# Left-side tile addresses, an opening with both pairs in turn, and a single reciprocal pass

## The chip, the core and the metric

The kernel runs on one core of one Trainium2 chip. The metric is the time of one execution on the device in microseconds (us). A core has a TensorE (matmul, "PE", with its weight loads listed apart as "PEld"), a VectorE ("DVE"), a ScalarE ("ACT"), a GpSimd ("POOL") and a SyncE ("SP"). SP and POOL issue most transfers here: what stands in one of these queues is issued in order, so a load that has to wait for its buffer holds up all loads behind it. Each engine, too, works through its own instructions in the order in which they were written.

## What is computed

`x` is 2048 x 640 in float32. A linear-attention block with 32 heads of 20 columns and a gated feed-forward block with 1536 inner columns are mixed row by row.

```python
def _A_ref(x, wqkv, wo):
    ...
    phi = lambda t: jnp.where(t > 0, t + 1, jnp.exp(t)) + 1e-6
    pq, pk = phi(q), phi(k)
    kv = jnp.einsum("bhsd,bhse->bhde", pk, v)
    z = jnp.einsum("bhsd->bhd", pk)
    num = jnp.einsum("bhqd,bhde->bhqe", pq, kv)
    den = jnp.einsum("bhqd,bhd->bhq", pq, z)[..., None] + 1e-6
    o = num / den
    return (lambda x, *d: x.transpose(*d))(o, 0, 2, 1, 3).reshape(B, S, D) @ wo

def _B_ref(x, w_gate, w_up, w_down):
    ...
    h = _sigmoid(g) * u
    return jnp.einsum("bsf,fd->bsd", h, w_down)

x = A_x
g = _sigmoid((x * gate_w).sum(-1, keepdims=True))
a = _A_ref(x, A_wqkv, A_wo)
b = _B_ref(x, B_w_gate, B_w_up, B_w_down)
return g * a + (1 - g) * b
```

## The kernel before

Every float32 product is made of three matmuls of rounded operands (`mm3`, lines 190 to 194): high times high, high times low, low times high. So every operand is split first (`split`, line 220): ACT writes the high half, DVE the low half, which is why nearly all instructions of the trace carry the helpers' lines 191 to 193 (PE), 203 (ACT) and 207 (DVE). In the names of the trace `h` and `l` at the end stand for the two halves. The products are formed by a Strassen-like scheme on 2 x 2 blocks with 7 products instead of 8 (the forms B11, B21, T1 to T4, B22).

The 2048 columns are four groups of 512; groups 2 and 3 make up pair 1, groups 0 and 1 pair 0. The work runs in stages:

- **k and the Gram-like sums** (0 to about 144 us), with the tile `gt` at its end.
- **The M stage** (144 to 180), woven into the q products. Heads are taken in six groups (`hg`: five of 120 columns, one of 40). `kv_part` multiplies `gt` with the loaded `wv_sb` and leaves `kvt`, split into `kvh` and `kvl`; `wo_split` splits a group's rows of `wo` into `woh` and `wol`; `m_part` multiplies the two and stores M to `m_dram`, from where the folded weights `mp_dram` are formed. The weights of q and of the feed-forward stage come as raw tiles `wst` (two buffers) through `load_w`, on the same SP queue as `wv_sb` and `wo_sb`.
- **q** (to about 215): its features p are stored to `p_dram`, and their small parts of the sum are made.
- **The feed-forward stage** (215 to 536): twelve steps f of 128 inner columns; both pairs in turn, pair 1 first. `FBlock` multiplies the sigmoid of the gate with the up product and (1 - g), stores the result tiles `c` in `h_dram` and forms their sums T1 to T4 (`turned`, `sums`). In the background the factor g / den is made (`fac_steps`): `den` sums p times z over the rows on DVE, `spread` sums it over the heads by a float32 matmul with `e_mat`, `one` takes the reciprocal, and p times the factor is stored as two further row blocks of `h_dram` and as the remainder `r_dram`. It is done for pair 1 at f=0 and 3, and for pair 0 at f=4 and 8.
- **The last stage** (536 to 766): the down product, in which the attention's p is treated as two more row blocks. A list `SEQ` gives the order of (pair, form); each has four chunks (`hw`, 128 x 1024, split into `hf`) and one set of weights: E (768 columns), O (1280), SE/SO (512 each, sums of E and O made on DVE by `sums` in `queue_down`), L and the remainder `hr` (loaded as `ot<-r`). Results are gathered in eight `ot` tiles and stored by POOL. The sums of the last f step come from `late_sums`, which loads T1, x, B21 and B22 back into four `ot` tiles.

What sets the order: a planner (`Order`) keeps modelled clocks of PE, ACT and DVE. Work for ACT and DVE is queued (`add`) with a cost, a key and a time from which it may run; `fill` emits queued items where the modelled clocks leave room, `need(key)` forces them out, `items` goes before `mid`, and `mid` before `lazy`. `after="p"` first fills and then lets the instruction wait for PE's modelled clock. In the last stage `plan` is the order in which weights (E, O, L, S), chunks (h), `late` and `r` are queued.

Tiles live in pools that grow from the left end or from the right end of the on-chip memory. The left-hand ones (`kp`, `m1`, `p1`, `mp`, `ha`, `pb`, `hb`) stand behind `common`, whose last tile is a placeholder named `space` (line 250) of 32 float32 numbers per partition. In the built program the left-hand operands begin at a multiple of 128 bytes, the right-hand ones (`px`, `pa`, `pg`, `xa`, `pw`, `wa`) at 96 modulo 128. In the last stage the chunks `hf` are on the left and the weights `wa` on the right; in the feed-forward stage pair 0's inputs are partly on the left and pair 1's on the right.

Of the kernel before, what the change touches and what calls it, by code (L numbers as in the profile page):

```python
# [45 lines left out]
class Order:  # L46
# [122 lines left out]
def gated_mix_kernel(ctx: ExitStack, tc: tile.TileContext, xt, xn, wk, wv, wo, wst_q, wst_f, out_t):  # L169
# [74 lines left out]
    h_dram = {(pr, n): dram.tile([P, FC // 2 + 2, TG], F32, name=f"h{pr}{n}") for pr in range(2) for n in FORMS}  # L244
    x_dram = [dram.tile([P, TG], F32, name=f"x{pr}") for pr in range(2)]
# [4 lines left out]
    common.tile([P, 32], F32, name="space")  # L250
# [407 lines left out]

    def load_w():
        if w_loads:  # L660
            n = kind, i = w_loads.pop(0)
            t = pg.tile([P, 2, D], F32, name="wst", tag="wst", bufs=2)
            if kind == "f":
                nc.sync.dma_start(t, wst_f[i, :, 0:2])
            elif kind == "q":
                nc.sync.dma_start(t, wst_q[:, 2 * (i % 2):2 * (i % 2) + 2])
# [389 lines left out]
    def wo_split(hg):  # L1056
        _, w = hg_slice(hg)
        woh = mp.tile([bdn, D], F32R, name="woh", tag="woh", bufs=2)
        wol = mp.tile([bdn, D], F32R, name="wol", tag="wol", bufs=2)
# [4 lines left out]
    def queue_wo(hg):  # L1064
        if hg < NHG:
            order.add(a_cost(D), v_cost(D), lambda: wo_split(hg), ("wo", hg), lambda: MO_AT[hg], first=True)

    def kv_part(hg):
# [3 lines left out]
        for m in range(KC):  # L1072
# [6 lines left out]
        act(kvh[:w, :w], kvt[:w, :w], AF.Copy, "v")  # L1079
        KV[hg] = (kvh, kvl)  # L1080
        order.add(0, v_cost(bdn), lambda: vec2(kvl[:w, :w], kvt[:w, :w], f32(kvh[:w, :w]), OP.subtract), ("kv", hg),
                  first=True)
        load_mv(hg + 3)

    def m_part(hg):
        c0, w = hg_slice(hg)
        order.need(("kv", hg))
# [9 lines left out]
        queue_wo(hg + 2)  # L1097
# [8 lines left out]
    load_mv(2)  # L1106
    load_mo(0)
    load_mo(1)

# [14 lines left out]
    def m_close():  # L1124
# [8 lines left out]
        nt.queue_sums(last=False)  # L1133

# [6 lines left out]
    def gate_row(g):  # L1141
        return l_dram.rearrange("a b -> (a b)")[g * TG:(g + 1) * TG].partition_broadcast(P)
# [28 lines left out]
    queue_wo(1)  # L1171
    queue_wo(0)
# [66 lines left out]
    class FBlock(Block):  # L1239
# [47 lines left out]
        def late_sums(self):  # L1287
# [3 lines left out]
            for n, t in zip(names, tiles):  # L1291
                nc.sync.dma_start(t, h_dram[self.pr, n][:, self.p] if n else x_dram[self.pr])
            self.turned(*tiles, lambda at=order.pe + 16.0: at)


    def fac_steps(pr):

        st = {}
        gs = (2 * pr, 2 * pr + 1)

        def load_pair(n):
            g, u = gs[n // 3], 2 * (n % 3)
            w = min(2, KC - u)
            t = st["b"][:, 2 * (n % 2):2 * (n % 2) + w]
            nc.sync.dma_start(t, p_dram[:, u:u + w, g])
            st[n] = max(order.pe, order.vec) + 6.0

        def den(n, k):
            td = st["a"][:, n // 3]
            p = st["b"][:, 2 * (n % 2) + k % 2]  # L1310
            if k == 0:
                vec1(td, p, zcol[:, 0:1], zeps[:, 0:1], OP.mult, OP.add)
            else:
                vec3(td, p, zcol[:, k:k + 1], td, OP.mult, OP.add)
            if k in (1, 3, 4) and n + 2 < 6:
                load_pair(n + 2)

        def begin():
            st["a"], st["b"] = h_tile(), h_tile()
            load_pair(0)  # L1320
            load_pair(1)
            for n in range(6):
                for k in range(2 * (n % 3), min(2 * (n % 3) + 2, KC)):
                    order.add(0, v_cost(TG), lambda n=n, k=k: den(n, k), ("den", pr), lambda n=n: st[n], lazy=True)

        def spread(n):

            order.need(("den", pr))
            ps = ps_tile("dd")
            td = st["a"][:, n]  # L1330
            nc.tensor.matmul(ps, e_mat, td, start=True, stop=True)
            order.on_pe(4, TG)
            vec1(td, ps, EPS, op0=OP.add, after="p")
            gt_ = st["b"][:, n]
            nc.sync.dma_start(gt_, gate_row(gs[n]))
            at = order.pe + 5.0
            for j in range(4):
                cs = slice(j * P, (j + 1) * P)

                def one(cs=cs):  # L1340
                    order.on_vec(5 * P, "")
                    nc.vector.reciprocal(td[:, cs], td[:, cs])
                order.add(0, 0.85, one, lazy=True)

            def fin():
                act(gt_, gt_, AF.Sigmoid)
                vec2(td, td, gt_, OP.mult, "a")
            order.add(a_cost(TG), v_cost(TG), fin, ("fac", pr, n), lambda: at, lazy=True)

        def load_q(j):  # L1350

            for n in range(2):
                t = st["b"][:, 2 * n:2 * n + 2]
                if j < 2:
                    nc.sync.dma_start(t, p_dram[:, 2 * j:2 * j + 2, gs[n]])
                else:
                    nc.sync.dma_start(t[:, 0], p_dram[:, KC - 1, gs[n]])
            st["at"] = order.pe + 6.0

        def store(name, j, k):  # L1360
            nc.gpsimd.dma_start(h_dram[pr, name][:, FC // 2 + j], st["b"][:, k])

        def scale(j, n, k):
            t = st["b"][:, 2 * n + k]
            vec3(t, t, EPS, st["a"][:, n], OP.add, OP.mult)
            if j == 2:
                nc.gpsimd.dma_start(r_dram[pr][:, n], t)
            elif n == 0:
                store(("B11", "B21")[k], j, k)
            elif k:  # L1370
                store("B22", j, 3)
                st["at2"] = order.pe + 7.0

        def sums(j, k):
            b11, b21, b12, b22 = (st["b"][:, i] for i in range(4))
            name, i, out, x, y = (("T1", 0, b11, b12, b11), ("T3", 2, b12, b22, b12), ("T2", 3, b22, b22, b11),
                                  ("T4", 1, b21, b21, b22))[k]
            sub(out, x, y)
            store(name, j, i)

        def queue_prep():
            for j in range(3):
                order.add(0, 0, lambda j=j: load_q(j), lazy=True)
                for n in range(2):
                    for k in range(2 if j < 2 else 1):
                        order.add(0, v_cost(TG), lambda j=j, n=n, k=k: scale(j, n, k), ("prep", pr), lambda: st["at"],
                                  lazy=True)
                if j < 2:
                    for k in range(4):
                        order.add(0, v_cost(TG), lambda j=j, k=k: sums(j, k), ("prep", pr), lambda: st["at2"], lazy=True)  # L1390

        def two():
            spread(0)
            spread(1)
            queue_prep()

        return [lambda: order.add(0, 0, begin, lazy=True), two]


    hooks = {}  # L1400
    for pr, fs in ((1, (0, 3)), (0, (4, 8))):
        for f, fn in zip(fs, fac_steps(pr)):
            hooks.setdefault(f, []).append(fn)
    PP = (FC // 2 + 2) // 2
# [9 lines left out]
    def raw_down(odd, pp):  # L1414

        if pp < PP - 1:
            f = 4 * pp + odd
            return wst_f[f:f + 3:2, :, 2].rearrange("f p (o c) -> p f o c", c=P)
        return mp_dram[:, odd:odd + 3:2].rearrange("p f (o c) -> p f o c", c=P)

    def load_down(key, t=None):
# [3 lines left out]
        if kind == "S":  # L1425
            v = t[:, :8 * P].rearrange("p (j o c) -> p j o c", j=2, c=P)
            for j in range(2):
                nc.sync.dma_start(v[:, j], raw_down(j, n // 2)[:, n % 2, :4])
# [10 lines left out]
    d_loads = [("E", pp) for pp in range(1, PP)] + [("O", pp) for pp in range(PP)] + [("L", 0)]  # L1439
# [6 lines left out]
    def queue_down(key):  # L1446
# [4 lines left out]

        def sums():
            v = RAW[key][0]
            (e0, e1), (o0, o1) = ((v[:, j, 0::2], v[:, j, 1::2]) for j in range(2))
            add(o1, e1, o1)
            sub(e1, e0, e1)
            sub(e0, o1, e0)
            sub(o0, o0, e0)
# [20 lines left out]
        if kind == "S":  # L1479
            order.add(0, 4 * v_cost(2 * P), sums, None, at)  # L1480
            for j in range(2):
                order.add(a_cost(4 * P), v_cost(4 * P), lambda j=j: s_part(j), ("wa", ("SE", "SO")[j], n // 2))
# [6 lines left out]
    SEQ = [(1, "B11"), (1, "B21"), (1, "T4"), (0, "B11"), (0, "B21")]  # L1489
    SEQ += [(pr, n) for pr in (1, 0) for n in ("T2", "T1", "T3", "B22")] + [(0, "T4")]  # L1490
# [319 lines left out]
```

## Time and profile before

| what | value |
|---|---|
| runs (us) | 771.77, 772.05, 776.09; median 772.05 |
| profiled execution | 772.33 us, of which the profile's span is 770.5 us |
| mean granted clock of TensorE in it | 0.993 |
| matrix engine busy | 97% of the span |
| moved by transfers | 136.06 MB, 177 GB/s in the mean |

The page of the profile gives busy times, the chain of work that ended last, the costliest groups of instructions with their mean duration, and transfers. The prediction quotes from it and from finer views of the same trace: the table of windows (what each engine did in a stretch), the timeline (one row per instruction: start, duration, engine, line, operation, result <- operands, and in brackets the idle time ahead of it with what ended it; rows named SPq are the queue's own waiting and issuing), and the list of waits. Durations of a matmul in the timeline (0.39 us at 512 columns) overlap with the next one; the pace is read from the starts.

These are the two groups with the longest waits on the page's list of groups:

```profile
L191 PE MATMUL cc<-hf,wa 128*128 128x512 f32 x80 | 32.2, 403 | 1.3 <-ACT hf L203 1.3
...
L192 PE MATMUL cc<-hf,wa 128*128 128x512 f32 x80 | 32.3, 404 | 2.1 <-DVE hf L207 2.1
```

### The profile page before, as it was taken

To read this page: it belongs to the slowest core of one execution; us is meant where nothing else is said; L and a number is where in the kernel's file an instruction comes from. 1 tells how busy PE (TensorE), PEld (TensorE's weight loads), DVE (VectorE), ACT (ScalarE), POOL (GpSimd) and SP (SyncE) were. 2 spreads that over 40 slices of the span, in tenths; PEclk is the share of its full clock that TensorE was granted. 3 is DMA by queue.
4 is the path that set the end of the run, shared out by engine and by line. 5 is a ranking of instruction groups with operands and counts; after the bars stand their busy time and mean duration, and the time that the engine had idled before them with its cause. 6 is when DMAs were issued, how large, how long until landed. Compare 5 with 4: busy or idle time off the path is not lost.

```text
span 770.5 us, 9772 instructions
## 1 busy us (share of the span) xinstructions
PE 747.3 (97%) x3560; PEld 624.5 (81%) x3560; DVE 502.1 (65%) x802; ACT 321.5 (42%) x544; POOL 109.1 (14%) x192
## 2 busy tenths in 40 slices
PE   9999999979899999999999999999789998999998
PEld 7999999868687888788888878887567876888886
DVE  4877577765754667678887699776479593544340
ACT  5664545355666333332333234223264454424320
POOL 0210101011211012013131121241100000010000
PEclk9999999999999999999999999999999999999999
DMA  7553536766535423256465335477878567666431
GB/s 255 123 152 70 137 89 185 199 188 196 192 136 198 144 89 129 70 170 237 172 200 209 138 108 187 177 255 238 279 257 278 187 214 254 221 202 213 134 112 69
DMA packets 59909, 136.06 MB, mean 177 GB/s; under 512 B 10238, under 2 KB 23310, under 8 KB 59861
## 3 DMA queue, kind: packets, MB, share of 16 engines
q1 hardware_dynamic: 43109, 85.88, 34.6%
q0 software_dynamic: 16608, 49.43, 19.7%
q8 instruction: 28, 0.46, 0.2%
q14 instruction: 20, 0.16, 0.1%
q10 hardware_dynamic: 144, 0.13, 0.1%
HBM read 87.11 MB, written 44.70 MB: 171 GB/s over the span
## 4 chain that ended last, share of the span: by engine, by line
PE 75%; DMA 8%; DVE 7%; issue 5%; ACT 3%; SPq 1%; POOL 1%; ACTq 0%; DVEq 0%; POOLq 0%
PE cc L192 7%; PE cc L193 7%; PE cc L191 7%; PE rot L191 7%; PE rot L192 7%; PE rot L193 7%; PE ch L192 6%; PE ch L193 6%; PE ch L191 6%; PE dd L193 5%; PE dd L191 5%; PE dd L192 5%; DMA ot<-r 2%; DMA ws<-wst_f 2%; DVE hf L207 2%
## 5 line engine op out<-in xcount | busy, mean ns | idle before, releaser
L207 DVE TENSOR_TENSOR hf<-hw,hf 128x1024 fp32r<-128x1024 f32 x54 | 65.4, 1223 | 59.3 <-ACT hf L203 59.1
L203 ACT ACTIVATE hf<-hw 128x1024 fp32r<-128x1024 f32 x54 | 56.1, 1054 | 60.8 <-PE rot L193 28.9
L207 DVE TENSOR_TENSOR c<-cc,c 128x512 f32<-128x512 f32 x56 | 37.5, 686 | 48.0 <-PE cc L193 43.5
L203 ACT ACTIVATE wG<-wst 128x640 fp32r<-128x640 f32 x17 | 12.4, 736 | 73.9 <-PE dd L193 73.3
L203 ACT ACTIVATE c<-ch 128x512 f32<-128x512 f32 x32 | 19.2, 598 | 57.3 <-PE ch L193 55.3
L191 PE MATMUL dd<-xrh,wG 128*128 128x512 f32 x90 | 35.5, 395 | 0.0
L193 PE MATMUL dd<-xrh,wG 128*128 128x512 f32 x90 | 35.2, 391 | 0.0
L192 PE MATMUL dd<-xrl,wG 128*128 128x512 f32 x90 | 35.2, 391 | 0.0
L192 PE MATMUL cc<-hf,wa 128*128 128x512 f32 x80 | 32.3, 404 | 2.1 <-DVE hf L207 2.1
L207 DVE TENSOR_TENSOR c<-c,om 128x512 f32<-128x512 f32 x48 | 33.2, 692 | 1.7
L193 PE MATMUL dd<-hf,wa 128*128 128x512 f32 x80 | 31.9, 399 | 2.1 <-DVE wa L207 2.1
L191 PE MATMUL dd<-hf,wa 128*128 128x512 f32 x80 | 31.8, 397 | 2.0 <-ACT wa L203 2.0
L191 PE MATMUL cc<-hf,wa 128*128 128x512 f32 x80 | 32.2, 403 | 1.3 <-ACT hf L203 1.3
L191 PE MATMUL cc<-xbh,wS 128*128 128x512 f32 x84 | 32.8, 390 | 0.0
L193 PE MATMUL cc<-xbh,wS 128*128 128x512 f32 x84 | 32.7, 389 | 0.0
L192 PE MATMUL cc<-xbl,wS 128*128 128x512 f32 x84 | 32.7, 389 | 0.0
L1608 POOL DMA_DIRECT2D out_t<-ot x18 | 9.7, 540 | 159.0 <-DVE ot L207 155.5
L193 PE MATMUL cc<-hf,wa 128*128 128x512 f32 x80 | 32.2, 402 | 0.0
L192 PE MATMUL rot<-pkl,xnh 128*128 128x320 f32 x102 | 31.7, 310 | 0.0
L192 PE MATMUL dd<-hf,wa 128*128 128x512 f32 x80 | 31.7, 396 | 0.0
L191 PE MATMUL rot<-pkh,xnh 128*128 128x320 f32 x102 | 31.6, 309 | 0.0
L193 PE MATMUL rot<-pkh,xnl 128*128 128x320 f32 x102 | 31.4, 308 | 0.0
(485 smaller groups left out, 2240.0 us busy)
## 6 DMA issues: line engine op xcount, KB each, us to landing
hf<-p_dram SPq DMA_DIRECT2D x16, 512.0 KB, 4.6
hw<-h1T SPq DMA_DIRECT2D x16, 512.0 KB, 4.6
hw<-h0T SPq DMA_DIRECT2D x16, 512.0 KB, 4.1
wst<-wst_f SPq DMA_DIRECT2D x12, 640.0 KB, 4.2
xst<-xt SPq DMA_DIRECT2D x10, 640.0 KB, 7.5
hw<-h0B SPq DMA_DIRECT2D x12, 512.0 KB, 4.9
h1T<-c POOLq DMA_DIRECT2D x21, 256.0 KB, 2.6
h0T<-c POOLq DMA_DIRECT2D x21, 256.0 KB, 2.8
```

Of the source, the lines that this page charges most:

```text
L191: nc.tensor.matmul(out, l_hi, r_hi, start=first, stop=False, skip_group_check=True)
L192: nc.tensor.matmul(out, l_hi, r_lo, start=False, stop=False, skip_group_check=True)
L193: nc.tensor.matmul(out, l_lo, r_hi, start=False, stop=last, skip_group_check=True)
L203: nc.scalar.activation(out, src, fn, **kw)
L207: nc.vector.tensor_tensor(out, a, b, op=op)
L1608: (eng or nc.gpsimd).dma_start(out_t[o * P:(o + 1) * P, g * TG + c0:g * TG + c1], t[:, c0:c1])
```

## The change

1. **Addresses.** `space` shrinks from 32 to 24 float32 numbers, so that all left-hand tiles stand 32 bytes lower. Of the 2,512 matmuls with 512 columns in the program, 1,218 had one operand at 0 and the other at 96 modulo 128 bytes; after it 4 have differing ones.
2. **M stage ("q's small parts" and the weights).** The second raw weight load of q (`("q", 1)`) is held until the first two `wv_sb` and `wo_sb` loads are issued, and `("u", 0)` until the loads of the last x tiles (`release_w`). `wv_sb` has two buffers instead of three; `woh` and `wol` three instead of two; the splits of `wo` are queued in the order of the groups; `kvh` is cast on DVE instead of ACT.
3. **One factor pass.** `begin` at f=0 and `den_all` at f=3 treat all four groups at once: four spreads into 32 rows each of one tile, four reciprocals in place of sixteen, then the factor is stored (`f_dram`) and loaded again per pair.
4. **Sums of the S weights** are formed in the feed-forward stage (`load_s`, `sum_s`), stored (`s_dram`) and loaded ready-made in the last stage.
5. **Opening of the last stage.** `SEQ` begins with B11 of both pairs in turn: each E weight is used for a chunk of pair 1 and of pair 0. The late loads go on POOL's queue, both pairs' at the opening; x is stored before the last c tiles; the plan has E1, two chunks, E2 and so on. The copies out of psum wait without `fill` (`"q"`), and B21's results come by an ACT copy and an addition.

```diff
+        if "q" in after:
+            t = self.pe
...
-    common.tile([P, 32], F32, name="space")
+    common.tile([P, 24], F32, name="space")
...
+    w_hold, w_skipped = {("q", 1), ("u", 0)}, []
+    def release_w(n):
+        w_hold.discard(n)
+        if w_skipped:
+            w_skipped.pop()
+            load_w()
...
-            v = mp.tile([P, KC, bdn], F32, name="wv_sb", tag="wv_sb", bufs=3)
+            v = mp.tile([P, KC, bdn], F32, name="wv_sb", tag="wv_sb", bufs=2)
...
-        act(kvh[:w, :w], kvt[:w, :w], AF.Copy, "v")
+        vec_copy(kvh[:w, :w], kvt[:w, :w])
+        vec2(kvl[:w, :w], kvt[:w, :w], f32(kvh[:w, :w]), OP.subtract)
...
-                nc.sync.dma_start(t, h_dram[self.pr, n][:, self.p] if n else x_dram[self.pr])
-            self.turned(*tiles, lambda at=order.pe + 16.0: at)
+                nc.gpsimd.dma_start(t, h_dram[self.pr, n][:, self.p] if n else x_dram[self.pr])
+            self.turned(*tiles, lambda at=order.pe + 30.0: at)
...
+    def sum_s(p):
+        e, o = (st["a"][:, 2 + j].rearrange("p (o k c) -> p k o c", k=2, c=P) for j in range(2))
+        (e0, e1), (o0, o1) = ((t[:, 0], t[:, 1]) for t in (e, o))
+        add(o1, e1, o1)
+        sub(e1, e0, e1)
+        sub(e0, o1, e0)
+        sub(o0, o0, e0)
+        nc.gpsimd.dma_start(s_dram[p], st["a"][:, 2:4])
...
+    def den_all():
+        for n in range(NG):
+            spread(n)
+        den_out()
+        queue_s()
+    hooks = {0: begin, 3: den_all}
...
-    SEQ = [(1, "B11"), (1, "B21"), (1, "T4"), (0, "B11"), (0, "B21")]
-    SEQ += [(pr, n) for pr in (1, 0) for n in ("T2", "T1", "T3", "B22")] + [(0, "T4")]
+    SEQ = [[(1, "B11"), (0, "B11")], [(1, "B21")], [(1, "T4")], [(0, "B21")]]
+    SEQ += [[(pr, n)] for pr in (1, 0) for n in ("T2", "T1", "T3", "B22")] + [[(0, "T4")]]
...
-    REST, REST_AT = {}, {12: 0, 20: 1, 36: 0}
+    REST, REST_AT = {}, {16: 0, 20: 1, 36: 0}
...
+                if not nxt:
+                    nc.gpsimd.dma_start(x_dram[b.pr], old[i].c12)
...
-    plan = [("E", 1), ("h", 2), ("E", 2), ("h", 3), ("E", 3), ("late", 0), ("O", 0), ("h", 4), ("O", 1), ("h", 5), ("O", 2), ("h", 6),
-            ("O", 3), ("h", 7), ("L", 0), ("r", 1)]
+    plan = [("E", 1), ("h", 2), ("h", 3), ("E", 2), ("h", 4), ("late", 0), ("E", 3), ("h", 5), ("late", 1), ("O", 0),
+            ("h", 6), ("O", 1), ("h", 7), ("O", 2), ("h", 8), ("O", 3), ("h", 9), ("L", 0)]
...
+        if turn == [(0, "T4")]:
+            jobs = [(i, q, pp) for i in range(1) for q in (0, 1, None) for pp in range(PP)]
+        else:
+            jobs = [(i, q, pp) for pp in range(PP) for i in range(len(now)) for q in (0, 1, None)]
```

What this does to the order of the queues shows at three places. On SP at the passage to the M stage (about 135 to 160 us of the trace), before; `wst_q` are q's raw weights, `xt` x's raw tiles:

```order
L668 DMA wst<-wst_q 128x640
L666 DMA wst<-wst_q 128x1280 x3
L1021 DMA wv_sb<-wv 128x5x120 x3
L1028 DMA wo_sb<-wo 120x640 x2
L325 DMA xst<-xt 128x5x256 x2
L1021 DMA wv_sb<-wv 128x5x120
L1028 DMA wo_sb<-wo 120x640 x2
```

and after:

```order
L682 DMA wst<-wst_q 128x640
L680 DMA wst<-wst_q 128x1280
L1035 DMA wv_sb<-wv 128x5x120 x2
L1042 DMA wo_sb<-wo 120x640 x2
L680 DMA wst<-wst_q 128x1280
L329 DMA xst<-xt 128x5x256 x2
L1035 DMA wv_sb<-wv 128x5x120
L1042 DMA wo_sb<-wo 120x640 x2
```

Two `wv_sb` and two `wo_sb` loads now stand ahead of a weight load that they stood behind; the third `wv_sb` comes later. On ACT in the M stage (about 163 to 176 us), before:

```order
L203 ACTIVATE kvh<-kvt 120x120
L203 ACTIVATE ms<-rot 120x320 x2
L203 ACTIVATE c<-ch 128x512
L203 ACTIVATE kvh<-kvt 40x40
L203 ACTIVATE woh<-wo_sb 120x640 x2
L203 ACTIVATE wS<-wst 128x640
L203 ACTIVATE xbh<-xst 128x3x256
L203 ACTIVATE ms<-rot 120x320 x2
```

and after:

```order
L205 ACTIVATE ms<-rot 120x320 x2
L205 ACTIVATE woh<-wo_sb 120x640 x2
L205 ACTIVATE c<-ch 128x512
L205 ACTIVATE ms<-rot 120x320 x4
L205 ACTIVATE woh<-wo_sb 40x640
L205 ACTIVATE wS<-wst 128x640
```

The casts of `kvh` are gone from ACT, and the two `woh` splits stand ahead of the copy of `ch`. On SP at the opening of the last stage (from about 528 us), before; the `c` and `hw` loads are chunks, `ws` raw weights, `ot` late tiles:

```order
L1499 DMA c<-h1B_80 128x512 x4
L1502 DMA hw<-h1B_80 128x1024 x2
L1502 DMA hw<-h1B_81 128x1024
L1436 DMA ws<-wst_f 128x3x128 x4
L1292 DMA ot<-h1T_83 128x512
L1292 DMA ot<-x_88 128x512
L1292 DMA ot<-h1B_81 128x512
L1292 DMA ot<-h1B_85 128x512
L1436 DMA ws<-mp_dram 128x3x128 x2
L1502 DMA hw<-h1B_81 128x1024
```

and after:

```order
L1535 DMA c<-h1B_80 128x512 x2
L1535 DMA c<-h0B_73 128x512 x2
L1538 DMA hw<-h1B_80 128x1024
L1538 DMA hw<-h0B_73 128x1024
L1538 DMA hw<-h1B_80 128x1024
L1481 DMA ws<-wst_f 128x3x128 x4
L1481 DMA ws<-mp_dram 128x3x128 x2
L1538 DMA hw<-h0B_73 128x1024
```

The chunks alternate between the pairs, and the four late loads no longer stand between the weights E2 and E3.

More of the change, by code (lines that the diff above doesn't have):

```diff
@@ new lines, in begin, with spread @@
+    def begin():
+        st["a"], st["b"] = h_tile(), h_tile()
+        load_pair(0)
+        load_pair(1)
+        for n in range(12):
+            for k in range(2 * (n % 3), min(2 * (n % 3) + 2, KC)):
+                order.add(0, v_cost(TG), lambda n=n, k=k: den(n, k), ("den", n // 6), lambda n=n: st[n], lazy=True)
+    def spread(n):
+        g = DEN[n]
+        order.need(("den", n // 2))
+        ps = ps_tile("dd")
+        nc.tensor.matmul(ps, e_mat, st["a"][:, n], start=True, stop=True)
+        order.on_pe(4, TG)
+        rows = slice(g * H, (g + 1) * H)
+        act(st["b"][rows, 2], ps[rows], AF.Copy, "p", bias=EPS)
+        nc.sync.dma_start(st["b"][rows, 3], gate_row(g, H))
```

444 lines of the change are left out of this document (218 added, 226 removed).

## The prediction

> **What bounds the kernel now.** I read the page first (busy shares), then a table by stage, then the idle times of TensorE in the trace, and last what those idle times were waiting for.
>
> ```profile
> span 770.5 us, 9772 instructions
> PE 747.3 (97%) x3560; PEld 624.5 (81%) x3560; DVE 502.1 (65%) x802; ACT 321.5 (42%) x544; POOL 109.1 (14%) x192
> ```
>
> TensorE is busy for 747.3 of 770.5 us, so only 23.2 us are idle; anything beyond that has to come from the pace of the matmuls. The table by stage gives, per stretch, busy time and instruction count of PE, PEld, DVE, ACT and POOL, the granted clock, the DMA share and GB/s:
>
> ```profile
> 144.00:180.00 36.00, 31.16 (x174) 25.53 (x173) 21.47 (x44) 20.40 (x42) 4.59 (x8) 0.95 0.71 199
> 180.00:215.00 35.00, 32.24 (x132) 24.82 (x132) 22.96 (x32) 21.30 (x38) 7.53 (x14) 0.95 0.56 194
> 215.00:330.00 115.00, 115.00 (x497) 92.91 (x496) 73.03 (x121) 48.53 (x85) 14.17 (x27) 1.00 0.37 128
> 330.00:460.00 130.00, 130.00 (x564) 105.53 (x563) 103.39 (x171) 42.24 (x74) 29.50 (x55) 1.00 0.52 179
> ...
> 536.00:560.00 24.00, 18.17 (x74) 13.27 (x72) 12.48 (x16) 7.02 (x9) 3.22 (x6) 1.00 0.68 236
> 560.00:600.00 40.00, 38.01 (x154) 29.97 (x155) 32.86 (x47) 20.76 (x28) 3.23 (x6) 0.96 0.81 277
> ...
> 640.00:660.00 20.00, 17.32 (x73) 13.44 (x73) 11.49 (x12) 9.57 (x12) 1.62 (x3) 1.00 0.72 246
> ...
> 700.00:766.00 66.00, 66.00 (x284) 53.09 (x283) 20.30 (x19) 18.11 (x20) 2.70 (x5) 1.00 0.38 128
> ```
>
> The feed-forward stage (215 to 536) has no idle PE at all; the idle time sits in 144 to 215, in the opening of the last stage (536 to 600) and at 640 to 660. The clock was below 1 in three stretches: 0.95 of 36 us, 0.95 of 35 us, 0.96 of 40 us, each about 1.6 us lost.
>
> **The change part by part.** The profiled execution took 772.33 us (0.28 above the median, 772.05); the sum is made against it.
>
> *Address of the left side's tiles.* Shrinking the placeholder moves every tile of the left-hand pools by 32 bytes, so that hf, and pair 0's inputs in the feed-forward stage, lie at 96 modulo 128 bytes as the weights in the right-hand pools do. The program has 3520 matmuls before and after. What an address is worth can be seen where pair 1 (right side, 96 against 96) is followed by pair 0 (left side, 0 against 96) with the same weights, in the timeline of TensorE (start, duration):
>
> ```profile
> 303.35 0.39 PE L191 MATMUL rot<-xt3h,wU 128*128 128x512 f32 x1
> ...
> 305.39 0.40 PE L191 MATMUL rot<-xt3h,wU 128*128 128x512 f32 x1
> ...
> 307.49 0.39 PE L191 MATMUL dd<-xrh,wG 128*128 128x512 f32 x1
> ...
> 639.82 0.39 PE L191 MATMUL dd<-hf,wa 128*128 128x512 f32 x1
> ...
> 642.39 0.40 PE L193 MATMUL dd<-hf,wa 128*128 128x512 f32 x1
> ```
>
> Nine matmuls of pair 1 take 2.04 us (227 ns each), nine of pair 0 2.10 us (233 ns), and the eleven steps of the last stage from 639.82 to 642.39 take 234 ns each. That is 6.6 ns a matmul. The stage table gives less: 215 to 460 is 245 us for 1061 records, 230.9 ns with two pairs of slow fp32 spreads in it (1.88 us and four records each, a row further down; 229.1 without them), and 700 to 766 is 232.4; with a quarter of the first and nine tenths of the second in the mixed kind, that is 3.3/0.67 = 4.9 ns. I take 5.5, between them. By the addresses in the built program 1,218 of 2,512 matmuls with 512 columns are of the mixed kind (856 of them in the last stage, 305 in the feed-forward stage), and 4 are left by the change: 1,218 x 5.5 ns = **-6.7 us**, with 6.0 to 8.0 as ends.
>
> The Trainium skill, "TensorE: Matmul & The Clock Gate", section "Back-to-back issue gap", gives the warm step by the number of columns alone (215.7 ns at 512), and "Advanced Engine Details and Errata", section "SBUF Cachelines", knows lines of 16 bytes, on which 0 and 96 both begin. By these this term would be 0. No step here is as short as 215.7 ns, and the rows just shown differ at the same column count, so I go with the rows.
>
> *M stage (144 to 180).* The idle times of TensorE that the change touches are these (the bracket holds the idle time ahead of the instruction and its releaser), with the SP queue's rows behind the first:
>
> ```profile
> 148.61 1.28 PE L1073 MATMUL rot<-gt,wv_sb 128*120 128x120 f32 x10 [0.50 <-DMA wv_sb<-wv]
> ...
> 170.80 0.40 PE L191 MATMUL rot<-woh,kvh 120*120 120x320 f32 x1 [1.80 <-ACT woh L203]
> ...
> 171.96 0.41 PE L192 MATMUL rot<-wol,kvh 120*120 120x320 f32 x1 [0.76 <-DVE wol L207]
> ```
>
> ```profile
> 135.52 8.39 SPq L666 DMA_DIRECT2D wst<-wst_q  x2
> 144.00 1.52 SPq L1021 DMA_DIRECT2D wv_sb<-wv  x3
> ```
>
> The second wst load waits on SP until 143.9 for its buffer, and wv stands behind it. Held back, it lets wv start some 8 us earlier: 0.50 goes. With wo splits in order and a third buffer, group 2's split no longer runs behind group 3's at 169.4 to 170.8: 1.80 and 0.76 go, and with them, I think, the 1.6 us of slow clock that follow. That is 4.7. Against it stand the places that become late next. With two buffers the fifth wv load is queued on SP behind a wo load that waits for a split, and on VectorE two low halves of wo (0.82 each, as the 128x640 splits here) now stand ahead of one kvt of the matrix product: I book 1.0 for each, and 0.7 for the longer chain of kvh on VectorE. **-2.0**, ends -4.7 and +0.7 (the new waits double). The dead time at 206 to 211, behind the stores of M and of p, keeps its order on all queues: 0, give or take 1.5.
>
> *Feed-forward stage.* Four spreads at f=3 instead of two and two; 4 reciprocals instead of 16; the factor stored and loaded again (16 loads of 32 rows); the 32 sums of the S weights moved here from the last stage.
>
> ```profile
> L207 DVE TENSOR_TENSOR ws<-ws 128x256 f32<-128x256 f32 x33 | 14.0, 423 | 0.8
> ...
> L1342 DVE RECIPROCAL hf<-hf 128x128 f32<-128x128 f32 x16 | 13.9, 917 | 0.1
> ...
> 318.43 1.88 PE L1331 MATMUL dd<-hf,e_mat 128*128 128x512 f32 x4
> ...
> L203 ACT ACTIVATE c<-ch 128x512 f32<-128x512 f32 x32 | 19.2, 598 | 57.3 <-PE ch L193 55.3
> ```
>
> VectorE gives back 12 x 0.917 = 11.0 us and takes 32 x 0.423 = 13.5; at 103 of 130 us in its fullest stretch it has room. The sums bring sixteen loads of 256 KB and eight stores of 512 KB, 8.4 MB over some 200 us or 42 GB/s, on top of 128 to 179, far from the 277 reached at 560. The work is hidden by a TensorE that is full for 321 us. What may show is the third spread: dd has two buffers, so it waits for ACT's copy of the first. The row has two spreads in 1.88 us, so the second covers 0.94 us of that copy (a 128x512 copy by ACT takes 0.60 in the last row) and little is left: **+0.3**, ends 0 and +3 (a late last denominator).
>
> *Opening of the last stage (536 to 592).* TensorE's idle times, and the SP rows behind them:
>
> ```profile
> 542.53 0.51 PE L193 MATMUL dd<-hf,wa 128*128 128x512 f32 x1 [1.82 <-DVE wa L207]
> ...
> 552.75 0.50 PE L191 MATMUL dd<-hf,wa 128*128 128x512 f32 x1 [1.99 <-ACT wa L203]
> ...
> 553.75 0.50 PE L193 MATMUL dd<-hf,wa 128*128 128x512 f32 x1 [0.26 <-DVE wa L207]
> ...
> 559.00 0.50 PE L191 MATMUL cc<-hf,wa 128*128 128x512 f32 x1 [1.25 <-ACT hf L203]
> ...
> 560.72 0.50 PE L192 MATMUL cc<-hf,wa 128*128 128x512 f32 x1 [1.22 <-DVE hf L207]
> ...
> 571.85 0.50 PE L192 MATMUL cc<-hf,wa 128*128 128x512 f32 x1 [0.90 <-DVE hf L207]
> ...
> 591.46 0.51 PE L192 MATMUL ch<-hf,wa 128*128 128x512 f32 x1 [0.38 <-DVE hf L207]
> ```
>
> ```profile
> 532.41 0.34 SPq L1292 DMA_DIRECT2D ot<-h1T  x1
> ...
> 545.42 0.34 SPq L1292 DMA_DIRECT2D ot<-x  x1
> 546.82 1.09 SPq L1436 DMA_DIRECT2D ws<-mp_dram  x2
> ...
> 541.52 0.95 DVE L207 TENSOR_TENSOR wa<-ws,wa 128x768 fp32r<-128x768 f32 x1
> ```
>
> The idle times add to 7.8; each matmul ahead of one is shown 0.39 long while the step is 0.23, so each of the seven hides another 0.16: 9.0 us, and 1.6 of slow clock (0.96 of 40 us) makes 10.6. From 532 to 545 SP stood at the load of x, whose store had not been issued, and E3 was asked for only at 546.8. In the new program the late loads are POOL's, x is stored before the last c tiles, and each E weight serves two chunks. A chunk has 18 matmuls, 4.1 us: TensorE first ran dry at the end of pair 1's chunk 0, at about 540.3 (542.53 - 1.82 less two steps of 0.23), so the second chunk on the same weight takes it to 544.4, and E1's low half, behind the same ten c operations on VectorE, is done at 542.5; E3 is needed at 561 and O0 at 569, some 15 us after their loads can go out. So every one of the seven waits has its cover. Not all is free: both pairs' late loads take all eight ot tiles, and the copy of pair 1's first small sum needs one back before its psum buffer is wanted again at about 572 (the third product of chunk 8). The sums that free them stand on VectorE behind the splits of four O weights and of chunk 9. No row shows such a wait; the nearest are the seven above, of 0.4 to 2.2 us, so I leave one of the longest kind and a bit, 2.4 us: **-8.2**, ends -10.6 and -3.
>
> *The wait at 642.*
>
> ```profile
> 635.18 7.87 DMA ot<-r
> ...
> 641.68 0.63 ACT L203 ACTIVATE hr<-ot 128x512 fp32r<-128x512 f32 x1 [5.30 <-DMA ot<-r]
> ...
> 644.70 0.50 PE L191 MATMUL ch<-hf,wa 128*128 128x512 f32 x1 [1.91 <-ACT hf L203]
> ...
> 645.96 0.50 PE L192 MATMUL ch<-hf,wa 128*128 128x512 f32 x1 [0.76 <-DVE hf L207]
> ```
>
> ACT sat at the split of r, whose second load took 7.87 us amid other transfers, and three hf splits stood behind it. 1.91 + 0.76 + 2 x 0.16 = 3.0 us. The S loads come earlier and ready-made, and pair 0's late loads are gone from here. I take **-2.3**, ends 0 and -3.
>
> *Sum:* 772.33 - 6.7 - 2.0 + 0.3 - 8.2 - 2.3 = 753.4 us.
>
> **The rivals.** *A, addresses are worth nothing:* 753.4 + 6.7 = 760.1. For it: DMA and other engines differ between the two stretches. Against it: the 227 and 233 ns stand side by side within 4 us. The two sections of the Trainium skill named above would have it come out this way. *B, the opening is bound by the transfers.* Until 572 it moves ten h chunks and six weights (some 8 MB), late tiles in and out (3.6 MB) and the last stores (2 MB), 13.6 MB; at the 277 GB/s seen from 560 to 600 that is 49 us against 36, and if half of the 13 us too many falls on TensorE, 6.5 us of stalls stay instead of 2.4, and the 1.6 of slow clock with them: a gain of 2.5 instead of 8.2, 759.1. Against it: the O weights past O0 and the late sums' stores are not needed by then. *C, slower than before:* the late loads now sit on POOL's queue behind stores that wait for VectorE. VectorE runs in order, so while the late sums wait, splits of chunk 10 and of L wait too and TensorE stops with them. Each us that the late tiles land after about 563 costs one. To end over 1% slower (780) they would have to land 26 us after that, 46 us after POOL gets to them at 543; the slow r load needed 7.87. *D, the opening and the addresses both give half or less, and the M stage nothing:* about 765, no change that can be measured.
>
> **How the numbers follow.** About 1% (7.7 us) is what a measurement of this kernel tells from no change, so the borders are 764.3 and 779.8. Forecast 0.62; A 0.12 and B 0.16, both faster; D 0.07; C 0.03. Faster is 0.62 + 0.12 + 0.16 = 0.90, the same 0.07, slower 0.03. The range: every term at its better end gives 772.33 - 8.0 - 4.7 - 10.6 - 3.0 = 746.0; upward it takes in A and B each by itself and stops at 764, just short of both together (765.8) and of D.
>
> **What would show it.** Addresses: the steps of pair 0 at f of any number, and of hf with wa, at 227 to 229 ns; 700 to 766 shrinks by 1.5 us or more for the same records. M stage: no idle time before woh and wol near 170, and a clock of 1.00 there. Opening: no SP wait on x, E3 asked for before 545, no idle PE before 569, clock 1.00; a wait of rot or cc on ACT's ot copy at 570 to 575 would be the remainder booked. At 642: no wait for hr. The prediction is wrong if hf with wa stays at 234 ns, or if TensorE waits for hf or wa between 545 and 600 for over 6 us in sum.

## The result and the profile after

The changed kernel takes 769.45 us in the median of its 16 runs, the kernel before 775.41 us in the median of as many on the same chip: a ratio of 0.9928, with a 95% interval of 0.9904 to 0.9951. That is a gain of 5.6 us where 18.9 were forecast. One run of the changed kernel, 777.72 us at a granted clock of 0.981, counts as a slow one and is left out of the ratio. The profiled execution of the changed kernel took 771.51 us (span 769.7 us), in the upper part of its runs; the other fifteen lie between 764.9 and 772.9, and the time goes with the granted clock: the four runs at 0.993 took 764.9 to 768.4, the four at 0.986 to 0.988 took 769.2 to 772.8. So the mean clock of one and the same kernel differs from run to run, and single spans say less here than pieces of the trace.

The table of windows of the changed kernel, TensorE first, with the clock, DMA share and GB/s at the end, for the same stretches as before:

```profile
144.00:180.00 36.00, 31.94 (x182) 26.48 (x181) 23.28 (x53) 18.53 (x34) 4.44 (x8) 0.95 0.73 210
180.00:215.00 35.00, 31.19 (x127) 24.40 (x126) 21.80 (x30) 19.31 (x35) 7.54 (x14) 0.93 0.53 183
215.00:330.00 115.00, 114.90 (x491) 92.30 (x490) 74.76 (x126) 50.47 (x88) 13.47 (x25) 0.99 0.45 153
330.00:460.00 130.00, 130.00 (x571) 106.81 (x570) 102.92 (x179) 43.40 (x76) 34.44 (x64) 1.00 0.62 217
...
536.00:560.00 24.00, 24.00 (x106) 19.55 (x105) 13.89 (x17) 7.26 (x9) 6.40 (x12) 1.00 0.76 268
560.00:600.00 40.00, 31.11 (x121) 24.30 (x120) 27.27 (x30) 24.57 (x33) 3.22 (x6) 0.87 0.77 269
...
640.00:660.00 20.00, 19.67 (x85) 15.69 (x84) 9.33 (x9) 10.46 (x12) 0.00 (x0) 1.00 0.55 183
...
700.00:766.00 66.00, 65.98 (x284) 53.16 (x283) 20.02 (x19) 18.53 (x21) 2.70 (x5) 1.00 0.39 128
```

Three things are to be seen. From 536 to 560 TensorE is now full, as forecast; but 560 to 600 holds 31.11 us of work where it held 38.01, at a clock of 0.87 instead of 0.96: what the opening won, it lost a little later. From 640 to 660 the wait is gone. And 700 to 766 has 284 matmul records in 66 us, exactly as many as before: the pace of the last stage hardly moved.

The list of waits of TensorE in the changed kernel (total, times, longest) names the new place:

```profile
PE rot L193 <- ACT ot L205: 7.7, 1, 7.7
PE rot L193 <- ACT ms L205: 2.6, 3, 1.1
PE rot L1088 <- ACT qr L205: 2.2, 1, 2.2
```

The first is longer than any wait before the change. Its story can be read from the timeline, engine by engine: ACT, then VectorE, POOL, ACT again, and TensorE.

```profile
560.03 1.27 ACT L205 ACTIVATE wa<-ws 128x1280 fp32r<-128x1280 f32 x1 [6.53 <-DMA ws<-wst_f]
...
571.78 1.28 ACT L205 ACTIVATE wa<-ws 128x1280 fp32r<-128x1280 f32 x1 [3.13 <-DMA ws<-mp_dram]
...
574.50 1.22 DVE L209 TENSOR_TENSOR hf<-hw,hf 128x1024 fp32r<-128x1024 f32 x1
575.63 3.70 DVE L209 TENSOR_TENSOR ot<-ot 128x512 f32<-128x512 f32 x6
...
576.62 0.54 POOL L1266 DMA_DIRECT2D h1T<-ot  x1 [28.55 <-DVE ot L209]
...
582.23 0.60 ACT L205 ACTIVATE ot<-rot 128x512 f32<-128x512 f32 x1 [2.82 <-DMA h1T<-ot]
...
574.80 0.40 PE L195 MATMUL ch<-hf,wa 128*128 128x512 f32 x1
582.88 0.79 PE L193 MATMUL rot<-hf,wa 128*128 128x512 f32 x1 [7.68 <-ACT ot L205]
583.47 0.63 PE L194 MATMUL rot<-hf,wa 128*128 128x512 f32 x1
583.90 0.63 PE L195 MATMUL rot<-hf,wa 128*128 128x512 f32 x1
```

VectorE works in order. The late sums (the six `ot<-ot`) stand behind the four O splits and chunk 9, and the last O weight, whose load waits for a `ws` buffer, reaches ACT only at 571.78. So the sums start at 575.63, their stores at 576.62, and the copy of pair 1's small sum, which needs an `ot` tile back from those stores, at 582.23. TensorE, which wants the psum buffer of that small sum at about 575, stands for 7.68 us, and the clock is about halved behind it (0.43 us from 583.47 to 583.90), for twelve steps or 2.3 us. (The granted clock was 0.50 from 580 to 583 already, within the wait; so the 0.87 in the table of windows is lower than these twelve steps alone would make it.)

### The profile page after: what moved, and what is told of

The parts are those of the page before. It is cut to its first block, busy times and chain, and to the rows that moved or that the text cites. A ratio compares the mean times of both kernels' runs of the same rounds, so it can differ in the third digit from the quotient of the medians.

```text
span 769.7 us, 9816 instructions
## 1 busy us (share of the span) xinstructions
PE 745.7 (97%) x3560; PEld 626.8 (81%) x3560; DVE 489.7 (64%) x789; ACT 322.7 (42%) x543; POOL 118.0 (15%) x209
## 4 chain that ended last, share of the span: by engine, by line
PE 60%; issue 15%; DMA 5%; ACT 3%; DVE 2%; POOL 1%; POOLq 0%; ACTq 0%
PE cc L193 6%; PE cc L194 6%; PE cc L195 6%; PE rot L193 5%; PE rot L194 5%; PE rot L195 5%; PE ch L194 5%; PE ch L195 5%; PE ch L193 5%; PE dd L193 4%; PE dd L194 4%; PE dd L195 4%; DMA m_dram<-ms 1%; DMA xst<-xt 1%; DMA xnst<-xn 1%
## 5 line engine op out<-in xcount | busy, mean ns | idle before, releaser
L193 PE MATMUL dd<-xrh,wG 128*128 128x512 f32 x90 | 36.8, 409 | 0.3 <-ACT dd L205 0.3
L195 PE MATMUL dd<-xrh,wG 128*128 128x512 f32 x90 | 36.1, 402 | 0.0
L193 PE MATMUL rot<-hf,wa 128*128 128x512 f32 x64 | 25.9, 405 | 8.0 <-ACT ot L205 7.7
L193 PE MATMUL ch<-hf,wa 128*128 128x512 f32 x80 | 32.5, 406 | 0.7 <-ACT ot L205 0.7
L194 PE MATMUL dd<-hf,wa 128*128 128x512 f32 x80 | 31.7, 396 | 1.2 <-DVE hf L209 1.2
L194 PE MATMUL ch<-hf,wa 128*128 128x512 f32 x80 | 32.2, 402 | 0.0
L205 ACT ACTIVATE c<-rot 128x512 f32<-128x512 f32 x24 | 14.4, 598 | 42.4 <-PE rot L195 35.3
L195 PE MATMUL ch<-hf,wa 128*128 128x512 f32 x80 | 32.0, 400 | 0.0
L193 PE MATMUL dd<-hf,wa 128*128 128x512 f32 x80 | 31.7, 396 | 0.0
```

What stands on the lines that cost most here:

```text
L193: nc.tensor.matmul(out, l_hi, r_hi, start=first, stop=False, skip_group_check=True)
L194: nc.tensor.matmul(out, l_hi, r_lo, start=False, stop=False, skip_group_check=True)
L195: nc.tensor.matmul(out, l_lo, r_hi, start=False, stop=last, skip_group_check=True)
L205: nc.scalar.activation(out, src, fn, **kw)
```

## The experiments

Ratios are to the kernel before, with 95% intervals. A difference of two ratios times 775 us gives the price of an edit. The intervals are 0.004 to 0.012 wide, or 3 to 10 us, so a price of 2 or 3 us is a rough one unless the trace supports it.

**Addresses, one step further.** The left-hand tiles were moved by another 128 bytes:

```diff
-    common.tile([P, 24], F32, name="space")
+    common.tile([P, 56], F32, name="space")
```

> The changed kernel with the placeholder 32 numbers (128 bytes) larger still, so that left-hand tiles lie at 224 modulo 256 bytes, as the right-hand ones do; in the changed kernel they were at 96 modulo 256, equal to the right-hand ones only modulo 128. Theory (operands must agree modulo 256): the steps of hf with wa fall from 232 ns to about 228, pair 0's steps in the feed-forward stage fall to 228, and the kernel is about 1,218 x 4.4 ns = 5 us faster than the changed one, 0.986 of the kernel before. Rival (modulo 128 is all there is, and the last stage is slow for another reason): steps stay at 232 ns, ratio 0.993.

Measured: 763.35 us, 0.9874 (0.9843 to 0.9906), 4.2 us less than the changed kernel. The same stretch of the last stage, as starts of TensorE in the changed kernel and in this one (27 steps each):

```profile
675.66 0.39 PE L195 MATMUL ch<-hf,wa 128*128 128x512 f32 x1
...
681.94 0.39 PE L195 MATMUL ch<-hf,wa 128*128 128x512 f32 x1
```

```profile
675.66 0.39 PE L193 MATMUL rot<-hf,wa 128*128 128x512 f32 x1
...
681.78 0.39 PE L193 MATMUL ch<-hf,wa 128*128 128x512 f32 x1
```

6.28 us against 6.12, or 232.6 against 226.7 ns a step. In the feed-forward stage those products of pair 0 that had unequal addresses fell from 232 to 227 ns. The theory holds: equality modulo 128, which is all that the change had brought, is not enough, and equality modulo 256 is.

**Addresses, undone.** The changed kernel with the placeholder of before:

```diff
-    common.tile([P, 24], F32, name="space")
+    common.tile([P, 32], F32, name="space")
```

> The changed kernel with the placeholder of before (32 numbers), all else as changed. Theory: the steps of hf with wa go back from 232 to 234 ns, pair 0's feed-forward steps likewise, in all 2 to 4 us slower than the changed kernel (ratio to the kernel before 0.995 to 0.998). Rival (addresses matter nothing): steps stay at 232 ns and the ratio at 0.993.

Measured: 771.94 us, 0.9960 (0.9940 to 0.9981). The move that the change made is worth 0.0032, or 2.5 us; steps of hf with wa are 234.2 ns in the mean again, as in the theory. The two intervals overlap (0.9940 to 0.9951), but the steps say the same as the ratios: 1,218 times 1.8 ns is 2.2 us.

**The late sums earlier.** 

```diff
-            if k == 6:
+            if k == 4:
                 order.need(("sums", 1), False)
                 order.need(("sums", 0), False)
```

> The changed kernel with the late sums forced out two chunks earlier (ahead of chunk 4 instead of chunk 6), so that on VectorE they stand ahead of the four O splits instead of behind them. Theory (the 7.7 us wait at 575 to 583 is the copy of pair 1's first small sum waiting for an ot tile that the late sums hold, and the late tiles have long landed): that wait and the slow clock behind it go, 7 to 10 us faster than the changed kernel, ratio to before about 0.982. Rival (the late tiles or the stores are what is late): VectorE waits for the late tiles, the O splits wait behind it, and the wait of TensorE stays over 5 us at a new place, ratio about 0.99.

Measured: 762.60 us, 0.9858 (0.9815 to 0.9900), 5.4 us less than the changed kernel, somewhat under the 7 to 10 expected. In VectorE's timeline of this run the sums now stand ahead of the O splits:

```profile
551.14 1.89 DVE L209 TENSOR_TENSOR ot<-ot 128x512 f32<-128x512 f32 x3
553.82 1.90 DVE L209 TENSOR_TENSOR ot<-ot 128x512 f32<-128x512 f32 x3 [0.79 <-DMA ot<-h0B]
556.31 1.49 DVE L209 TENSOR_TENSOR wa<-ws,wa 128x1280 fp32r<-128x1280 f32 x1 [0.60 <-ACT wa L205]
```

The late tiles had landed by 553.8, so they were not what was late. The wait of 7.7 us is gone: TensorE's idle times from 536 to 600 are 2.2 us in sum, where they were 7.8 in the kernel before and 8.9 in the changed one. The transfers of this stretch ran no slower than before (314 GB/s against 268 in the changed kernel). What is left of the list of waits is smaller:

```profile
PE rot L1088 <- DMA wv_sb<-wv: 3.0, 1, 3.0
...
PE ch L193 <- ACT hr L205: 1.3, 1, 1.3
PE ch L193 <- ACT ot L205: 1.1, 1, 1.1
```

**The M stage put back.** The changed kernel with the M stage of before (cut to its core):

```diff
-    w_hold, w_skipped = {("q", 1), ("u", 0)}, []
+    w_hold, w_skipped = set(), []
...
-            v = mp.tile([P, KC, bdn], F32, name="wv_sb", tag="wv_sb", bufs=2)
+            v = mp.tile([P, KC, bdn], F32, name="wv_sb", tag="wv_sb", bufs=3)
...
-        woh = mp.tile([bdn, D], F32R, name="woh", tag="woh", bufs=3)
+        woh = mp.tile([bdn, D], F32R, name="woh", tag="woh", bufs=2)
...
-        vec_copy(kvh[:w, :w], kvt[:w, :w])
+        act(kvh[:w, :w], kvt[:w, :w], AF.Copy, "v")
...
-    for hg in range(3):
-        queue_wo(hg)
+    queue_wo(1)
+    queue_wo(0)
```

> The changed kernel with the M stage as it was before (no held weight loads, three wv buffers, two wo buffers, wo splits in the old order, kvh cast on ACT); all else as changed. Theory (the new M stage costs more than it brings: x's raw tiles come later behind the moved weight load, ms waits for its store): 135 to 215 us shrinks by 1.5 to 3 us and the kernel is that much faster than the changed one, ratio to before about 0.990. Rival (the M stage gained and the loss lies elsewhere): 2 us slower than the changed one, ratio about 0.996.

Measured: 771.29 us, 0.9978 (0.9952 to 1.0004). The theory falls: the new M stage is worth 0.0050 or 3.9 us, although the intervals touch. I had formed it from this wait of the changed kernel and the slow clock behind it:

```profile
159.79 1.28 PE L1088 MATMUL rot<-gt,wv_sb 128*120 128x120 f32 x10 [2.17 <-ACT qr L205]
```

The run shows the other side: its waits for `woh` and `wol` near 171 are back.

```profile
170.81 0.40 PE L193 MATMUL rot<-woh,kvh 120*120 120x320 f32 x1 [1.80 <-ACT woh L205]
171.98 0.54 PE L194 MATMUL rot<-wol,kvh 120*120 120x320 f32 x1 [0.76 <-DVE wol L209]
```

**Both repairs together.** The placeholder of 56 and the late sums ahead of chunk 4.

> The changed kernel with the placeholder of 56 numbers and the late sums ahead of chunk 4 together. Theory (the two losses are independent: steps of 232 instead of 227 ns, and the ot wait): the gains add, ratio 0.9874 x 0.9858 / 0.9928 = 0.980 of the kernel before, about 759 us. Rival (with the faster steps TensorE runs into transfers or splits that come too late): ratio 0.985 or more, and over 6 us of waits between 540 and 600.

Measured: 757.38 us, 0.9764 (0.9733 to 0.9794), better than either repair alone and at least the sum of the two gains (0.980, which carries the uncertainty of three ratios). TensorE's idle times from 540 to 600 are 3.7 us in sum, and the rival falls.

**A third wv buffer on top.**

```diff
-            v = mp.tile([P, KC, bdn], F32, name="wv_sb", tag="wv_sb", bufs=2)
+            v = mp.tile([P, KC, bdn], F32, name="wv_sb", tag="wv_sb", bufs=3)
...
-        woh = mp.tile([bdn, D], F32R, name="woh", tag="woh", bufs=3)
-        wol = mp.tile([bdn, D], F32R, name="wol", tag="wol", bufs=3)
+        woh = mp.tile([bdn, D], F32R, name="woh", tag="woh", bufs=2)
+        wol = mp.tile([bdn, D], F32R, name="wol", tag="wol", bufs=2)
...
-        load_mv(hg + 2)
+        load_mv(hg + 3)
...
-        queue_wo(hg + 3)
+        queue_wo(hg + 2)
...
     load_mo(1)
+    load_mv(2)
...
-    for hg in range(3):
+    for hg in range(2):
         queue_wo(hg)
```

> As the run with the 56-number placeholder and early sums, but with three wv buffers again (the third wv load stands right behind the first wo loads) and two wo buffers; the wo splits stay in order. Theory (the wait of 2 to 3.4 us near 157 is the third wv load, which with two buffers cannot be issued before the first product is done): that wait goes and with it the slow clock that follows, 2 to 4 us faster than without, about 756 us; woh waits stay under 1 us. Rival (that wait is x's raw tile, behind the moved weight load, or the wo splits need the third buffer): the wait near 157 stays, or one of the size comes back at woh near 170; no faster.

Measured: 757.74 us, 0.9774 (0.9751 to 0.9797): no faster. TensorE's idle times in this run:

```profile
156.63 1.31 PE L1088 MATMUL rot<-gt,wv_sb 128*120 128x120 f32 x10 [0.23 <-ACT lt L205]
...
172.27 0.40 PE L193 MATMUL rot<-woh,kvh 120*120 120x320 f32 x1 [1.56 <-ACT ms L205]
```

The wait near 157, which was 0.81 for `wv_sb` in the run without the third buffer, is down to 0.23, so there it was the third wv load. But 1.56 us stand near 172, where it was 0.58. They are put down to ACT's copy `ms`, not to `woh`, and on ACT that copy stood behind the split of a weight that had waited for VectorE:

```profile
171.15 0.74 ACT L205 ACTIVATE wS<-wst 128x640 fp32r<-128x640 f32 x1 [0.95 <-DVE wst L209]
171.80 0.42 ACT L205 ACTIVATE ms<-rot 120x320 f32<-120x320 f32 x1
```

TensorE's idle times from 150 to 185 are 4.1 us in sum here and 3.7 without the third buffer. The theory was right on the place and wrong on the gain. The rival was right that it is no faster; that the two wo buffers are the reason is not shown.

**The old M stage on top of both repairs.** The edit of the M stage put back, on the kernel with both repairs.

> As the run with the 56-number placeholder and early sums, but with the whole M stage as before the change. Theory (the new M stage loses as much at wv and ms as it gains at woh): within 1.5 us of the run with the new M stage, about 759 us. Rival (the new M stage is worth the 2 us that was predicted): 761 us or more.

Measured: 759.59 us, 0.9799 (0.9774 to 0.9825), against 0.9764: the new M stage is worth 0.0035 or 2.7 us here. The median lies between the 759 of the theory and the 761 of the rival, and the two intervals overlap. It is the second measurement of the same sign.

**The address alone, in the kernel before.** Its placeholder from 32 to 56 numbers and nothing else.

> The kernel before with nothing changed but the placeholder, from 32 to 56 numbers, so that both operands of all products with 512 columns agree modulo 256. Theory (234 ns becomes 227): 1,218 x 7.3 ns = 9 us faster than before, ratio about 0.988. Rival (only what stands ahead of TensorE changes, and the waits of the opening and of the M stage swallow it): ratio 0.993 or more.

Measured: 768.44 us, 0.9913 (0.9887 to 0.9939), 6.7 us. One line of the kernel before, set right, brings as much as the whole change did (5.6 us; the intervals overlap). Steps of hf with wa are 226.8 ns, as in the theory. The gain is less than the 9 us of the steps, and the interval still holds the rival's 0.993: the trace has slow clock at three places of the last stage (windows 0.93, 0.96 and 0.97), where there was one.

**Other distances.** The kernel with early sums, with placeholders of 40 and of 48 numbers (64 and 32 bytes from equality); one run each.

> The run with early sums, but a placeholder of 40 numbers: left-hand tiles at 160 modulo 256 bytes, 64 below the right-hand ones. Only the steps of hf with wa are read. Theory (only equality modulo 256 gives the fast step, any distance costs): 231 to 235 ns, like the distances of 96 and 128 seen so far. Rival (equality modulo 64 is enough, and 128 apart is a case by itself): 227 ns.

> The run with early sums, but a placeholder of 48 numbers: left-hand tiles at 192 modulo 256 bytes, 32 below the right-hand ones. Theory (only equality modulo 256 gives the fast step): 231 to 235 ns. Rival (the cost grows with the distance): clearly under 231, since 32 is the smallest distance tried.

Measured: 760.83 and 764.59 us; as single runs these times aren't compared. The stretch from 690 to 750 (TensorE's busy time and its records) in the kernel before, the changed one, and those with 40, 48 and 56 numbers:

```profile
690.00:750.00 60.00, 60.00 (x257) 1.00 0.47 153
```

```profile
690.00:750.00 60.00, 60.00 (x260) 1.00 0.48 153
```

```profile
690.00:750.00 60.00, 60.00 (x258) 1.00 0.41 133
```

```profile
690.00:750.00 60.00, 60.00 (x259) 1.00 0.42 137
```

```profile
690.00:750.00 60.00, 60.00 (x266) 1.00 0.42 140
```

Only the last gets more matmuls through, by 2 to 4%. The theory holds, and the rivals fall: neither equality modulo 64 nor a small distance is enough.

**The late loads back on SP's queue**, with both repairs kept (`nc.gpsimd` to `nc.sync` in `late_sums`).

> The run with early sums and 56 numbers, with the late loads put back on SP's queue, where they stand between the weights E2 and E3 as before the change. Theory (the move to POOL is needed: SP waits behind the stores of the last c tiles until about 541, and E3, the chunks and O0 come later): SP waits 5 us or more at the late loads and TensorE has 3 us more of waits between 545 and 575; ratio to before about 0.980 against 0.9764. Rival (the earlier store of x alone freed the queue): no difference.

Measured: 757.33 us, 0.9790 (0.9729 to 0.9852), with a median equal to that of the run with both repairs. SP does wait for the late loads, as the timeline of its queue shows:

```profile
528.42 0.34 SPq L1306 DMA_DIRECT2D ot<-h1T  x1
537.08 0.34 SPq L1306 DMA_DIRECT2D ot<-x  x1
...
542.01 0.91 SPq L1481 DMA_DIRECT2D ws<-mp_dram  x2
```

In the run with the late loads on POOL the same load of E3 is asked for 5.3 us earlier:

```profile
536.69 0.95 SPq L1481 DMA_DIRECT2D ws<-mp_dram  x2
```

So the first half of the theory came: SP is held up. The second did not: TensorE's idle times between 545 and 575 are 2.2 us in sum against 1.5. The rival's reason isn't borne out either, since SP still stands 8.2 us ahead of the load of x. The interval is too wide to exclude 2 us either way; that the move to POOL is needed isn't shown.

Not tried apart: the single factor pass with the S sums in the feed-forward stage, and the opening put back alone. TensorE's 130.00 of 130.00 and 114.90 of 115.00 us in the windows say that the first costs TensorE next to nothing there.

## Why the prediction was wrong

The terms of the sum and what the runs and the trace gave for them:

| term | forecast | measured | from |
|---|---|---|---|
| addresses | -6.7 | -2.5 | 0.9960 to 0.9928 |
| M stage | -2.0 | -3.9, and -2.7 on the repaired kernel | 0.9978 to 0.9928; 0.9799 to 0.9764 |
| feed-forward stage | +0.3 | not measured apart | 0.1 us idle in the windows |
| opening | -8.2 | about +0.9 | idle and slow clock, 10.6 to 11.5 |
| wait at 642 | -2.3 | about -1.7 | waits of 0.33 and 0.66 in place of 3.0 |

The measured terms add to -7.2, or -6.0 with the second price of the M stage; the ratio says -5.6, with an interval from -7.4 to -3.8. Two steps failed. The first is the sentence that tiles at 96 modulo 128 would lie "as the weights in the right-hand pools do". In the kernel before, every product with the fast step had operands equal modulo 256 (224 with 224, 128 with 128), and the slow ones were 128 with 224; modulo 128 and modulo 256 could not be told apart there. The change made 96 with 224, a case that no row of the trace showed. I priced it as the equal case (5.5 ns) and it brought 2. So the effect was real; the rival "worth nothing" gave too little and the forecast too much. The price itself was that of the equal case: from 32 to 56 numbers the changed kernel gains 0.0086 (0.9960 to 0.9874) and the kernel before 0.0087, both 6.7 us. That this is the very number of the forecast is in part luck, for the steps got 7.4 ns shorter and not 5.5. (Two readings behind the term were inexact: of the nine steps of pair 0 only the six of `xt3` have unequal addresses, and the program has 876 of the 1,218 in the last stage, not 856.) What would have helped is a list of the pairs of addresses that the trace really had, and the new pair as an unknown with 0 and 5.5 ns as its ends.

The second is the remainder in the opening. The mechanism was on record word by word: the ot tiles, the copy of pair 1's small sum, the psum buffer wanted "at about 572", the sums behind four O splits and chunk 9. Its size was not worked out but taken from unrelated waits: 2.4 us. Measured are 7.68 us of idle time and 2.3 of slow clock. A number that should have warned stood in the trace of the kernel before, in the row of VectorE's fourth O split:

```profile
571.71 1.48 DVE L207 TENSOR_TENSOR wa<-ws,wa 128x1280 fp32r<-128x1280 f32 x1
```

It ends at 573.2, after the 572 at which the psum buffer was wanted, and in the new order chunk 9, the sums, a store and a copy come behind it. In the changed kernel these links can be read: O weights go through two ws buffers, so the fourth load waits for the second split (the first two loads take some 10 us, asked for at 549 and 552, split at 560.03 and 562.62); the fourth split comes at 571.78, the sums (3.70 us) at 575.63, and the copy at 582.23. The run with early sums shows that this order alone cost 5.4 us of the time. None of the signs that the prediction had set for being wrong caught it: hf with wa stood at 232.4 ns and not at 234, and TensorE waited only 1.21 us for hf or wa between 545 and 600. The wait came at `ot`, which the prediction had listed as the remainder and left without a limit.

The other steps stood in the main. The seven waits of the opening are gone but for 1.21 us at 564, SP is not held at x, and E3 is asked for at 543.8. The M stage gained about what was forecast, but not by the route taken, so that its number came near is in part luck. The waits of `woh` and `wol` did go. The slow clock did not: 144 to 180 has 0.95 as before, where 1.00 was expected. And the 0.50 at the first wv load went, but a wait of 2.17 came at the third. The profile names ACT's copy `qr` for it, behind one of x's raw tiles; the two wv loads of that time took 8.7 and 9.1 us, the third from 150.95 on, so it landed at about the same time, and in the run with early sums the same wait (3.0) is put down to it. Which of the two ended last in the changed kernel stays open; I had booked 1.0 for a later wv load. At 642 the wait went. Of the rivals for the opening B came nearer than the forecast, with a gain of 2.5 where there was none, but by a cause that the runs don't show: with the sums earlier, more bytes a second were moved and the wait was gone, so it was not the bandwidth but the order on VectorE.

## What to carry to other kernels

Whoever hangs a gain on an address should list which residues (addresses modulo 128, 256 and so on) the trace has really shown together, and to what modulus they agree; a new pair of residues is an unknown, even if it is "more equal" than before. When a plan moves work behind a chain of loads with few buffers, the chain's end has to be worked out link by link (buffer, load, split, sum, store, copy), above all when the prediction has already named it; a wait that is named and not sized is the first to look for. And a wait can cost more than its own length: the one of 7.68 us was followed by 2.3 us of slow clock, while the two of 1.91 and 0.76 us near 645 in the kernel before were followed by none.

## What the runs showed of the hardware

The step from one matmul to the next with 512 columns depends on where in SBUF the moving operand and the weights begin. Steps from the traces, grouped by the addresses in the built programs (last stage, products of hf with wa):

| moving operand, weights (modulo 256 bytes) | mean step | kernel |
|---|---|---|
| 224, 224 | 226.9 ns | placeholder of 56 |
| 128, 128 | 227.9 ns | before (48 products) |
| 96, 96 | 228.1 ns | the change (48 products) |
| 192, 224 | 233.3 ns | placeholder of 48 |
| 160, 224 | 233.3 ns | placeholder of 40 |
| 128, 224 | 234.3 ns | before |
| 96, 224 | 232.4 ns | the change |

Equality is 2 to 3% faster; every distance tried costs 5.5 to 7.4 ns against 226.9, with no order by distance. It is not the moving operand's own address that counts: at 96, 128, 160 and 192 the step is short, 227.5 to 228.1 ns, where the weights begin there, too. Whether 256 is the modulus, or 512, isn't settled: the equal cases are equal to both. The Trainium skill, "Advanced Engine Details and Errata", section "SBUF Cachelines", has lines of 16 bytes, to which all these cases are alike; the runs show an effect at a coarser grain.
